# Both parts of z side by side in HBM and in the operand blocks, with block loads, stores and last rows in another order over the queues

## The chip, the cores and the metric

The kernel runs on one core of a Trainium2 chip. The metric is the device time of one execution in microseconds (us), as the median of several runs. Before the change it is 2041.6 us.

## What is computed

The reference first convolves x with h along the sequence, and then mixes tokens with two full matrices:

```python
Xf = np.fft.rfft(x, n=2 * S, axis=1); Hf = np.fft.rfft(h, n=2 * S, axis=0)
y = np.fft.irfft(Xf * Hf[None], n=2 * S, axis=1)[:, :S, :]      # x: (8, 5696, 128)
theta = y @ w_theta
zr, zi = y * np.cos(theta), y * np.sin(theta)
yr = np.einsum('ts,bsd->btd', w_tok_r, zr)                      # w_tok: (5696, 5696)
yi = np.einsum('ts,bsd->btd', w_tok_i, zi)
u = y + yr + yi
out = u + np.maximum(u @ w_ch, 0.0)
```

## The kernel before

**Stages.** From 0 to about 390 us of the span the convolution runs as a two-step FFT over eight groups (four pairs of batches, two halves of the channels). The token mixing follows. It takes up nearly all of the rest: TensorE multiplies transposed 128x128 pieces of w_tok with operand blocks of z that lie in SBUF, 512 columns (four batches of 128 channels) at a time.

**Phases.** A phase step (`phase_step`, which calls `phases_b`) takes one tile of 128 tokens and four batches. TensorE transposes y into the PSUM tile tpz (L688) and forms theta (L525 to L531); VectorE copies tpz into a place in the tile ring (L693), of which there are six; ScalarE makes the sine and the cosine (L536 to L538); VectorE makes the two products zi and zr (L549, L550), which lie side by side in one of seven tiles zz. The y tile is stored to y2_hbm (y_hbm in the profile, L694) and the products to z_hbm (L567, one DMA for every 64 tokens, 128 rows of 1024 bytes), or straight into an operand block (below). There are 22 steps for the first four batches, `steps0`, which run beside the end of the FFT, and 22 for the other four, `steps1`, which run between the first products of the mixing. Later tiles are worked off one by one beside the mixing ("background", `bg_phase`). There the two products lie in two tiles, red and mag, or c2 and c3, which also serve as accumulators, and are stored with two DMAs for every 64 tokens (L570).

**Operand blocks.** The tokens of a pass fall into 11 blocks j = 0 to 10. A block is a tile of 7 x 1024 bf16 per partition: four raw parts (M2, M6 of zr, M7, M5 of zi, each for one half q of the batches) and three sums (M3, M4, M1). Two further sums are made in place over M6 and M7 (`sum_ops`, L776, five VectorE operations of 128x1024 for each block). `load_b` reads a whole block with two DMAs, one for each part (L760), `load_b_half` the first half q of a block with two DMAs (L771). Block 0 lies in the tile ring, the others in pools that reuse the FFT's memory. For blocks 0 to 8 the half q = 0 comes by `load_b_half` from z_hbm, and the half q = 1 is written by `steps1` straight from zz to its home in the block (L563): even rows by a DMA on SP's queue, odd rows by a DMA on Pool's queue. Blocks 9 and 10 of the first pass come with `load_b` on SP's queue, once `steps1` is through (`open_mixing`). In the second pass all 11 blocks come with `load_b` on ScalarE's queue (ACT).

**Weights.** `load_w` brings a piece of w_tok with four DMAs on Pool's queue (L627) into one of six places in the tile ring; `pump` issues these loads as far as places are free. VectorE transposes the pieces (`w_t`, L838) and adds or subtracts some of them (`w_sum`, L847). `prepare` does that one stretch (up to three blocks) ahead of TensorE.

**Order.** A list scheduler sets the order of each engine's instructions by its own model of time, except where `manual_schedule` keeps an engine in program order: VectorE in the first pairs of both passes, and Pool (`late_order`) from the last FFT group to the half loads of blocks 0 to 6. These are called in one loop behind the FFT. After `late_order` closes, Pool's order is the scheduler's again.

**Pairs.** A pair is an output tile of each half of the rows. The first pairs of a pass are "classic": eight products of raw parts (L1167), pieces of which stand between the phase steps of `steps1`. The later pairs use seven products (M1 to M7, L1250) and add them into the accumulators c0 to c3 (L1257). The last 64 rows (tt None, L1137) are a narrow stage of four stretches. In the first pass it is second to last, in the second pass it comes second, right behind the first pair. There the sums of the blocks are made in step with the first pair: `safe` makes three of a block, `in_place` the other two; the ten of blocks 9 and 10 are made after the pair's last products and ahead of what `prepare` does for the second stretch of the last rows. Finished rows go through `u_stage` (ReLU branch, L915 to L930), which uses the single PSUM bank "misc" for the transposes (utp) and for the product (v), read by L927.

Of the kernel before, what the change touches and what calls it, by code (L numbers as in the profile page):

```python
# [23 lines left out]
def kernel(  # L24
# [20 lines left out]
    z_hbm_h = nc.dram_tensor("z_hbm", (2, 2, 11, 2, 4, 64, BD // 2), BF16, kind="Internal")  # L45
# [450 lines left out]
    def phases_b(ti, y_ap, b0, nb, yT, sb, th_pool, th_tag, zi_eng, turns=None, tags=("red", "mag"), m=P,  # L496
                 theta_ps=None, copy=None, home={}):
# [42 lines left out]
        if tags is None:  # L540
            k = zz_n[0] = (zz_n[0] + 1) % 7
            zz = fh.tile([P, 1024], F16, tag=f"hs{4 + k}", name="zz").bitcast(BF16).rearrange(
                "p (z n) -> p z n", z=2)
            zr, zi = zz[:, 0], zz[:, 1]
            sides["zz"] = zz
        else:
            zi = red.bitcast(BF16)[:, :n]
            zr = mag.bitcast(BF16)[:, :n]
# [4 lines left out]
        for e in range((m + 63) // 64):  # L553
# [7 lines left out]
            if tags is None and j in home:  # L561
                for r in range(2):
                    (nc.gpsimd if r else nc.sync).dma_start(  # L563
                        home[j][32 * i:32 * i + 32, :4096].rearrange("p (z q r n) -> p z q r n", z=2, q=2, r=2)[:, :, q_, r],
                        zz[e * 64 + r:e * 64 + 64:2])
            elif tags is None:
                nc.sync.dma_start(z_hbm[:, p_, j, q_, i].rearrange("z t n -> t z n"), zz[rows])  # L567
            else:
                for r, z in enumerate((zr, zi)):
                    nc.sync.dma_start(z_hbm[r, p_, j, q_, i], z[rows])  # L570
# [84 lines left out]
    def load_ya1(yt=None):  # L655
# [10 lines left out]
        else:  # L666
            for e in range(2):
                nc.gpsimd.dma_start(st[1][HD:, 2 + e, :],
                                    yt[64 * e:64 * e + 64].rearrange("p m n -> p (m n)")[:, :H])

    M2, M6, M7, M5, M1, M3, M4 = range(7)
    ORDER = (M3, M4, M5, M2, M1, M7, M6)
    home_of = {}

    def phase_step(ti, hh, store=nc.sync):
# [16 lines left out]
        def copy():  # L692
# [5 lines left out]
                 tags=None, copy=copy, home=home_of if hh else {})  # L698
# [15 lines left out]
    late_order = ExitStack()  # L714
# [28 lines left out]
    bpe = [ctx.enter_context(tc.tile_pool(name="bpool_e", bufs=1, side="right", reuse_waits="tile"))]  # L743
    bts_of = {0: [], 1: []}

    place_of = {}

    def new_b(j, pool):
        return ring["all"][:, WB:WB + BT] if j == 0 else pool.tile([P, BT], BF16, tag=f"b{j}", name=f"b{j}")

    def tile_b(p, j, pool):
        t_ = place_of.pop(j) if j in place_of else new_b(j, pool)
        bt = [t_[:, k * 1024:(k + 1) * 1024].rearrange("p (r n) -> p r n", r=2) for k in range(7)]
        bts_of[p].append(bt)
        return t_

    def load_b(p, j, pool, eng=nc.scalar):
        t_ = tile_b(p, j, pool)
        for z in range(2):
            sides["late"] = eng.dma_start(  # L760
                t_[:, z * 2048:(z + 1) * 2048].rearrange("p (q n) -> p q n", q=2),
                z_hbm[z, p, j].rearrange("q i (s r) n -> (i s) q (r n)", r=2))

    def home_pool(j):
        return bpe[0] if j < 7 else bpe[1] if j < NE else bp

    def load_b_half(j):

        t_ = home_of[j] = tile_b(0, j, home_pool(j))
        for z in range(2):  # L770
            nc.gpsimd.dma_start(t_[:, z * 2048:z * 2048 + 1024],  # L771
                              z_hbm[z, 0, j, 0].rearrange("i (s r) n -> (i s) (r n)", r=2))

# [18 lines left out]
    for j in range(7):  # L792
        load_b_half(j)
    for step in steps0:
# [8 lines left out]
    steps1 = [lambda ti=ti: phase_step(ti, 1, nc.gpsimd) for ti in  # L803
              [0, 5, 11, 16, 1, 6, 12, 17, 10, 21, 2, 7, 13, 18, 3, 8, 14, 19, 4, 15, 9, 20]]
# [3 lines left out]
    def open_mixing():  # L808
# [6 lines left out]
        load_b(0, NJ - 2, bp, nc.sync)  # L815
        sides["cs"] = [addend(0, n, t, h) for n, (t, h) in enumerate(((0, 1), (22, 0), (0, 0), (22, 1)))]
        load_b(0, NJ - 1, bp, nc.sync)
# [6 lines left out]
    def next_steps(n):  # L824
        for _ in range(min(n, len(steps1))):
# [3 lines left out]
            if not steps1:  # L829
                open_mixing()  # L830
# [482 lines left out]
```

## Time and profile before

| | us |
|---|---|
| median of 3 runs (2041.51 to 2042.7) | 2041.6 |
| the profiled execution | 2038.09 |
| its span, from first to last instruction | 2036.3 |
| PE busy in the span | 1948.2 |
| DVE (VectorE) busy | 1574.1 |
| POOL busy | 974.3 |
| ACT (ScalarE) busy | 654.7 |

The page of the profile counts an engine as busy while it executes instructions; DMA issues of SP and ACT are not in it, but those of Pool are. Its three DMA queues of interest are q0 (Pool's, 158.13 MB, 61.0% of the time of 16 DMA engines), q1 (SP's and ACT's, 140.25 MB, 24.1%) and q10 (11.54 MB, 1.6%). The granted clock of TensorE is 0.987 on average; in a stretch it is given as a share, 1.00 for full speed.

In the rows below, `L1167` is line 1167 of the kernel, `out<-in` names the tiles or tensors that an instruction writes and reads, `x6` counts the instructions merged into one row, and square brackets give the idle time before the first of them and what ended it.

### The profile page before, as it was taken

Reading aid. Unit: us, or ns where it says so; the run is one execution under the profiler, and the core shown is the slowest. Engines: PE = TensorE matmul, PEld = TensorE weight load, DVE = VectorE, ACT = ScalarE, POOL = GpSimd, SP = SyncE. Lnnn points to the kernel's source line nnn. Section 1 sums busy time; section 2 is a strip of 40 time slices with the busy share of each in tenths; the row PEclk is TensorE's granted clock in tenths of the full one; section 3 lists DMA queues with packets and bytes.
Section 4 is the critical chain, followed back from the end, with each engine's and each line's share of the span. In section 5 each row is a group of like instructions: output and inputs, shape, how many; then the busy total and the mean of one; then the engine's idle time right before and its main releaser. Section 6 shows DMA issues by size and latency. Waiting matters only on the chain.

```text
span 2036.3 us, 41470 instructions
## 1 busy us (share of the span) xinstructions
PE 1948.2 (96%) x15841; PEld 1074.5 (53%) x15841; DVE 1574.1 (77%) x2890; ACT 654.7 (32%) x1004; POOL 974.3 (48%) x1744
## 2 busy tenths in 40 slices
PE   5799999799999999999999998999999999999998
PEld 5688888654444444444444444444444444444444
DVE  8777778777788888888867668768677786777767
ACT  6788888862233323333300000111111111111111
POOL 8523321485353545454566454453544545354450
PEclk9899999899999999999999999999999999999999
DMA  9878975999798989999999799796977979788793
GB/s 117 62 84 124 88 83 167 255 268 186 161 174 179 174 171 167 181 167 181 165 176 154 117 251 220 127 154 125 154 134 138 155 128 154 129 153 140 133 156 85
DMA packets 491239, 312.56 MB, mean 153 GB/s; under 512 B 182983, under 2 KB 456007, under 8 KB 490055
## 3 DMA queue, kind: packets, MB, share of 16 engines
q0 software_dynamic: 322608, 158.13, 61.0%
q1 hardware_dynamic: 162448, 140.25, 24.1%
q10 hardware_dynamic: 5984, 11.54, 1.6%
q8 instruction: 124, 2.03, 0.4%
q14 instruction: 75, 0.61, 0.1%
HBM read 354.89 MB, written 90.82 MB: 219 GB/s over the span
## 4 chain that ended last, share of the span: by engine, by line
PE 67%; DVE 3%; DMA 3%; issue 1%; POOL 0%; ACT 0%; DVEq 0%; SPq 0%
PE m L1250 62%; DMA ring<-in_moe_w_tok_i_dram 2%; DVE c L1257 1%; PE utp L918 1%; PE v L925 1%; PE m L1254 1%; PE m L1137 1%; DVE b L776 1%; DVE wt L838 1%; PE tpz L866 0%; PE theta_ps L514 0%; POOL ring L627 0%; DMA wl<-in_moe_w_tok_i_dram 0%; DMA z_hbm<-mag 0%; DVE c L927 0%
## 5 line engine op out<-in xcount | busy, mean ns | idle before, releaser
L627 POOL DMA_DIRECT2D ring<-in_moe_w_tok_i_dram x720 | 388.2, 548 | 662.2 <-DVE wt L838 582.5
L627 POOL DMA_DIRECT2D ring<-in_moe_w_tok_r_dram x720 | 386.9, 549 | 122.6 <-DVE wt L838 64.2
L838 DVE STREAM_TRANSPOSE wt<-ring 128x384 f32<-128x384 f32 (+2 forms) x720 | 358.8, 523 | 103.2 <-PE m L1250 66.5
L1250 PE MATMUL m<-b,wt 128*128 128x512 bf16 x1640 | 388.4, 379 | 2.0 <-DVE wt L838 1.7
L1250 PEld LDWEIGHTS <-wt 128*128 128x128 bf16 x1804 | 176.0, 98 | 215.5 <-DVE wt L838 4.0
L1257 DVE TENSOR_TENSOR c<-c,m 128x512 f32<-128x512 f32 x412 | 265.3, 670 | 0.4 <-PE m L1250 0.4
L920 ACT ACTIVATE ring<-utp 128x512 bf16<-128x512 bf16 x85 | 50.8, 597 | 580.2 <-PE utp L918 580.2
L137 POOL DMA_DIRECT2D x<-in_x_dram x128 | 99.4, 798 | 141.5 <-PE ps L250 132.7
L420 PE MATMUL ps<-r_u,u_t 128*128 128x128 f16 x1024 | 125.2, 221 | 5.9 <-DVE u_t L400 2.9
L421 PE MATMUL ps<-r_v,v_t 128*128 128x128 f16 x1024 | 124.2, 220 | 0.3
L1167 PE MATMUL m<-b,wt 128*128 128x512 bf16 x480 | 112.8, 385 | 6.3 <-DMA b<-zz 2.8
L915 ACT ACTIVATE ub<-c 128x512 bf16<-128x512 f32 x88 | 55.1, 628 | 196.5 <-DMA ring<-in_moe_w_tok_i_dram 114.6
L421 PEld LDWEIGHTS <-v_t 128*128 128x128 f16 x1024 | 100.9, 99 | 5.2 <-issue 3.7
L420 PEld LDWEIGHTS <-u_t 128*128 128x128 f16 x1024 | 100.9, 99 | 3.9 <-DVE u_t L400 3.9
L398 ACT ACTIVATE xs<-ps 128x1024 f16<-128x1024 f32 x96 | 91.6, 983 | 9.6 <-PE ps L274 2.9
L400 DVE TENSOR_TENSOR u_t<-xs,hs 128x1024 f16<-128x1024 f16 x96 | 64.3, 670 | 32.1 <-ACT xs L398 29.9
L1167 PEld LDWEIGHTS <-wt 128*128 128x128 bf16 x528 | 51.1, 99 | 67.9 <-issue 4.8
L516 ACT ACTIVATE red<-theta_ps,magic 128x512 f32<-128x512 f32 (+1 forms) x46 | 31.6, 687 | 136.5 <-PE theta_ps L514 113.6
L268 PEld LDWEIGHTS <-w_t 64*128 64x128 f16 x3240 | 58.6, 100 | 23.6 <-issue 17.9
L868 ACT ACTIVATE ring<-tpz 128x512 bf16<-128x512 bf16 (+1 forms) x46 | 27.5, 597 | 130.8 <-PE tpz L866 113.7
L927 DVE SCALAR_TENSOR_TENSOR c<-v,c 128x512 f32<-128x512 f32 x88 | 59.9, 682 | 7.1 <-PE v L925 6.9
L400 DVE TENSOR_TENSOR v_t<-xs,hs 128x1024 f16<-128x1024 f16 x96 | 63.7, 664 | 0.0
(2934 smaller groups left out, 3816.1 us busy)
## 6 DMA issues: line engine op xcount, KB each, us to landing
ring<-in_moe_w_tok_r_dram POOLq DMA_DIRECT2D x352, 96.0 KB, 4.4
ring<-in_moe_w_tok_i_dram POOLq DMA_DIRECT2D x352, 96.0 KB, 4.7
ring<-in_moe_w_tok_r_dram POOLq DMA_DIRECT2D x352, 80.0 KB, 4.4
ring<-in_moe_w_tok_i_dram POOLq DMA_DIRECT2D x352, 80.0 KB, 3.9
cp_hbm<-c SPq DMA_DIRECT2D x88, 256.0 KB, 2.4
c<-cp_hbm SPq DMA_DIRECT2D x88, 256.0 KB, 4.5
out_dram<-c SPq DMA_DIRECT2D x88, 256.0 KB, 4.4
yy<-y_hbm SPq DMA_DIRECT2D x84, 128.0 KB, 2.4
```

Of the source, the lines that this page charges most:

```text
L137: nc.gpsimd.dma_start(x16[p0:p1, e, n0:n0 + 16, :HD], bass.AP(tensor=src.tensor, offset=src.offset + (p0 * N2 + n0) * D + dh * HD, ap=[[N2 ...
L268: nc.tensor.matmul(ps[:, e, j * HD:(j + 1) * HD], w_t2[rows, slot(e, c0 + j), N2 * (1 - ri):N2 * (3 - ri)], a_st["a"][rows, ri * K1 + c0 + ...
L398: nc.scalar.activation(xs[:, :, :, :ck], ps, AF.Copy)
L400: nc.vector.tensor_tensor(uv[r][:, :, :, c0:c0 + ck], xs[:, :, :, :ck], hv[:, r:r + 1].to_broadcast([P, 2, HD, ck]), op=mult)
L420: nc.tensor.matmul(o, u_t[:, at:at + P], r_u, start=True, stop=False)
L421: nc.tensor.matmul(o, v_t[:, at:at + P], r_v, start=False, stop=True)
L627: nc.gpsimd.dma_start(wb[32 * i:32 * i + 32, :ng, :nj * 64], bass.AP(tensor=a.tensor, offset=a.offset + row0 * S + p * H + i * QR + j0 * 6 ...
L838: nc.vector.transpose(wt.rearrange("p j t r -> p (j t r)").bitcast(F32).rearrange("p (j g t) -> p g j t", j=TJ, g=4)[:, :ng, :nj], wb[:, : ...
L927: nc.vector.scalar_tensor_tensor(c[:m], v[:m], 0.0, c[:m], op0=ALU.max, op1=ALU.add)
L1167: nc.tensor.matmul(ms[n // 2 * 2 + h], a[n][:, j, :, r], bts_of[p][jj][n % 2 * 2 + h][:, r, :], start=(n % 2 == 0 and jj == 0 and r == 0), ...
L1250: nc.tensor.matmul(ms[q], a[q][:, j, :, r], bts[jj][q][:, r, :], start=(jj == 0 and r == 0), stop=(jj == NJ - 1 and r == 1 and q not in left))
L1257: nc.vector.tensor_tensor(c, z, ms[q], op=op)
```

## The change

- z_hbm gets the two parts of a token side by side: rows of 2 x 512 bf16 (2048 bytes). A store of 64 tokens is one DMA with 64 such rows. An operand block holds its raw parts in the order (q, r, z, n) instead of (z, q, r, n); each raw part then is two runs of 512 with a distance of 1024. The background phases write both products into the tile red.
- `load_b` and `load_b_half` are one DMA each instead of two, with rows of 4096 bytes for every partition and half q. The even and the odd home rows of zz are 32 rows of 2048 bytes for each DMA.
- `load_b_half(0)` is called right behind the two ya loads of the last FFT group (in `load_ya1`), ahead of the yt stores; blocks 1 to 6 stay where they were.
- The first two steps of `steps1` store y on SP's queue instead of Pool's. The last of them sends its odd rows over ACT's queue.
- Pool is kept in program order (`pool_order`) from before `next_steps(2)` until `steps1` is through.
- `load_b` of blocks 9 and 10 goes over ACT's queue instead of SP's.
- In the second pass the ten sums of blocks 9 and 10 are made inside the first stretch of the last rows, behind `prepare` of the second one.

```diff
-    z_hbm_h = nc.dram_tensor("z_hbm", (2, 2, 11, 2, 4, 64, BD // 2), BF16, kind="Internal")
+    z_hbm_h = nc.dram_tensor("z_hbm", (2, 11, 2, 4, 64, 2, BD // 2), BF16, kind="Internal")
...
-            zr, zi = zz[:, 0], zz[:, 1]
             sides["zz"] = zz
         else:
-            zi = red.bitcast(BF16)[:, :n]
-            zr = mag.bitcast(BF16)[:, :n]
+            zz = red.bitcast(BF16).rearrange("p (z n) -> p z n", z=2)
+        zi, zr = zz[:, 0], zz[:, 1]
+        rows_of = zz.rearrange("p z n -> p (z n)")
...
                 for r in range(2):
-                    (nc.gpsimd if r else nc.sync).dma_start(
-                        home[j][32 * i:32 * i + 32, :4096].rearrange("p (z q r n) -> p z q r n", z=2, q=2, r=2)[:, :, q_, r],
-                        zz[e * 64 + r:e * 64 + 64:2])
-            elif tags is None:
-                nc.sync.dma_start(z_hbm[:, p_, j, q_, i].rearrange("z t n -> t z n"), zz[rows])
+                    (nc.sync if not r else odd_eng or nc.gpsimd).dma_start(
+                        home[j][32 * i:32 * i + 32, :4096].rearrange("p (q r w) -> p q r w", q=2, r=2)[:, q_, r],
+                        rows_of[e * 64 + r:e * 64 + 64:2])
             else:
-                for r, z in enumerate((zr, zi)):
-                    nc.sync.dma_start(z_hbm[r, p_, j, q_, i], z[rows])
+                nc.sync.dma_start(z_hbm[p_, j, q_, i].rearrange("t z n -> t (z n)"), rows_of[rows])
...
+            load_b_half(0)          # at the end of load_ya1(yt)
...
+        raw = t_[:, :4096].rearrange("p (q r z n) -> p q z r n", q=2, r=2, z=2)
+        bt = [raw[:, k % 2, 1 - k // 2] if k < 4 else
+              t_[:, k * 1024:(k + 1) * 1024].rearrange("p (r n) -> p r n", r=2) for k in range(7)]
...
-        for z in range(2):
-            sides["late"] = eng.dma_start(
-                t_[:, z * 2048:(z + 1) * 2048].rearrange("p (q n) -> p q n", q=2),
-                z_hbm[z, p, j].rearrange("q i (s r) n -> (i s) q (r n)", r=2))
+        sides["late"] = eng.dma_start(
+            t_[:, :4096].rearrange("p (q w) -> p q w", q=2),
+            z_hbm[p, j].rearrange("q i (s r) z n -> (i s) q (r z n)", r=2))
...
-        for z in range(2):
-            nc.gpsimd.dma_start(t_[:, z * 2048:z * 2048 + 1024],
-                              z_hbm[z, 0, j, 0].rearrange("i (s r) n -> (i s) (r n)", r=2))
+        nc.gpsimd.dma_start(t_[:, :2048], z_hbm[0, j, 0].rearrange("i (s r) z n -> (i s) (r z n)", r=2))
...
-    for j in range(7):
+    for j in range(1, 7):
         load_b_half(j)
...
-    steps1 = [lambda ti=ti: phase_step(ti, 1, nc.gpsimd) for ti in
-              [0, 5, 11, 16, 1, 6, 12, 17, 10, 21, 2, 7, 13, 18, 3, 8, 14, 19, 4, 15, 9, 20]]
+    order1 = [0, 5, 11, 16, 1, 6, 12, 17, 10, 21, 2, 7, 13, 18, 3, 8, 14, 19, 4, 15, 9, 20]
+    steps1 = [lambda ti=ti, n=n: phase_step(ti, 1, nc.sync if n < 2 else nc.gpsimd, nc.scalar if n == 21 else None)
+              for n, ti in enumerate(order1)]
...
-        load_b(0, NJ - 2, bp, nc.sync)
+        load_b(0, NJ - 2, bp)
...
-        load_b(0, NJ - 1, bp, nc.sync)
+        load_b(0, NJ - 1, bp)
...
             if not steps1:
+                pool_order.close()
                 open_mixing()
...
+                pool_order.enter_context(tc.manual_schedule(engines={mybir.EngineType.Pool}))
                 next_steps(2)
...
                 c_last = addend_last(p)
             a1, a2, sa = a
+            if p and first_of_pair:
+                for f in (safe, in_place):
+                    for j in range(3 * TJ, NJ):
+                        f(j)
...
-            elif turn == 3 * TJ:
-                for f in (safe, in_place):
-                    for j in range(3 * TJ, NJ):
-                        f(j)
```

More of the change, by code (lines that the diff above doesn't have):

```diff
@@ L496, in phases_b @@
     def phases_b(ti, y_ap, b0, nb, yT, sb, th_pool, th_tag, zi_eng, turns=None, tags=("red", "mag"), m=P,
-                 theta_ps=None, copy=None, home={}):
+                 theta_ps=None, copy=None, home={}, odd_eng=None):
         n = nb * D
@@ L669, in load_ya1, with new_b, tile_b, load_b @@
                                     yt[64 * e:64 * e + 64].rearrange("p m n -> p (m n)")[:, :H])
+            load_b_half(0)
+    bpe = []
+    bts_of = {0: [], 1: []}
+    place_of, home_of = {}, {}
+    def new_b(j, pool):
+        return ring["all"][:, WB:WB + BT] if j == 0 else pool.tile([P, BT], BF16, tag=f"b{j}", name=f"b{j}")
+    def tile_b(p, j, pool):
+        t_ = place_of.pop(j) if j in place_of else new_b(j, pool)
+        raw = t_[:, :4096].rearrange("p (q r z n) -> p q z r n", q=2, r=2, z=2)
+        bt = [raw[:, k % 2, 1 - k // 2] if k < 4 else
+              t_[:, k * 1024:(k + 1) * 1024].rearrange("p (r n) -> p r n", r=2) for k in range(7)]
+        bts_of[p].append(bt)
+        return t_
+    def load_b(p, j, pool, eng=nc.scalar):
+        t_ = tile_b(p, j, pool)
+        sides["late"] = eng.dma_start(
+            t_[:, :4096].rearrange("p (q w) -> p q w", q=2),
+            z_hbm[p, j].rearrange("q i (s r) z n -> (i s) q (r z n)", r=2))
+    def home_pool(j):
+        return None if j == 0 else bpe[0] if j < 7 else bpe[1] if j < NE else bp
+    def load_b_half(j):
+        t_ = home_of[j] = tile_b(0, j, home_pool(j))
+        nc.gpsimd.dma_start(t_[:, :2048], z_hbm[0, j, 0].rearrange("i (s r) z n -> (i s) (r z n)", r=2))
     M2, M6, M7, M5, M1, M3, M4 = range(7)
     ORDER = (M3, M4, M5, M2, M1, M7, M6)
-    home_of = {}
-    def phase_step(ti, hh, store=nc.sync):
+    def phase_step(ti, hh, store=nc.sync, odd_eng=None):
         st = sides["phases"]
@@ L697, in phase_step @@
         phases_b(ti, y_ap, 4 * hh, 4, yT, None, None, None, nc.vector, st["turns"], theta_ps=theta_ps,
-                 tags=None, copy=copy, home=home_of if hh else {})
+                 tags=None, copy=copy, home=home_of if hh else {}, odd_eng=odd_eng)
     tile_order = []
@@ L712, in with_load @@
         return both
-    late_order = ExitStack()
+    late_order, pool_order = ExitStack(), ExitStack()
     for g, (bp, dh) in enumerate(groups):
@@ L741 @@
     conv.close()
[L743 to L758, printed above, removed]
-        for z in range(2):
-            sides["late"] = eng.dma_start(
-                t_[:, z * 2048:(z + 1) * 2048].rearrange("p (q n) -> p q n", q=2),
-                z_hbm[z, p, j].rearrange("q i (s r) n -> (i s) q (r n)", r=2))
[L764 to L769, printed above, removed]
-        for z in range(2):
-            nc.gpsimd.dma_start(t_[:, z * 2048:z * 2048 + 1024],
-                              z_hbm[z, 0, j, 0].rearrange("i (s r) n -> (i s) (r n)", r=2))
+    bpe.append(ctx.enter_context(tc.tile_pool(name="bpool_e", bufs=1, side="right", reuse_waits="tile")))
     def sum_ops(bt):
```

## The prediction

> **What bounds the kernel now.** I read the page first, then the stretches of 20 us, then TensorE's waits, then the time lines of single engines around the worst stretches.
>
> ```profile
> span 2036.3 us, 41470 instructions
> PE 1948.2 (96%) x15841; PEld 1074.5 (53%) x15841; DVE 1574.1 (77%) x2890; ACT 654.7 (32%) x1004; POOL 974.3 (48%) x1744
> ```
>
> TensorE is the bound: 88 us of the span are not PE. From 560 to 1160 us and from 1300 us on every stretch shows 20.00 of 20 at clock 1.00, and nothing that the change touches there can shorten it. The gain must come out of a few stretches (columns: us, then busy us and instructions of PE, PEld, DVE, ACT, POOL; granted clock, DMA share, GB/s):
>
> ```profile
> 380.00:400.00 20.00, 12.89 (x130) 9.24 (x128) 15.92 (x31) 17.38 (x31) 8.04 (x15) 0.90 0.82 207
> 400.00:420.00 20.00, 18.66 (x146) 11.29 (x145) 14.77 (x28) 13.80 (x24) 14.32 (x27) 0.85 0.98 343
> ...
> 440.00:460.00 20.00, 15.07 (x73) 6.57 (x70) 13.76 (x26) 3.48 (x7) 16.47 (x31) 0.93 0.96 243
> 460.00:480.00 20.00, 19.98 (x103) 9.37 (x102) 12.52 (x24) 3.43 (x7) 8.17 (x16) 0.98 1.12 247
> ...
> 1240.00:1260.00 20.00, 17.62 (x97) 7.85 (x95) 18.75 (x36) 2.78 (x5) 9.60 (x18) 1.00 0.84 177
> 1260.00:1280.00 20.00, 17.16 (x114) 7.82 (x115) 12.63 (x28) 1.79 (x3) 12.67 (x24) 0.91 0.93 155
> ```
>
> What TensorE waits for in them (us in total, times, longest):
>
> ```profile
> PE m L1137 <- DVE out__18362 L847: 4.1, 1, 4.1
> ...
> PE m L1167 <- DMA b<-zz: 2.8, 1, 2.8
> PE m L1167 <- DMA ring<-z_hbm: 2.6, 1, 2.6
> PE m L1167 <- DVE wt L838: 2.1, 1, 2.1
> ```
>
> The single engines say why. Pool first (start, us), then VectorE:
>
> ```profile
> 386.89 1.06 POOL L452 DMA_DIRECT2D yt_hbm<-yt  x2
> 387.94 1.12 POOL L771 DMA_DIRECT2D ring<-z_hbm  x2
> 396.02 0.55 POOL L694 DMA_DIRECT2D y_hbm<-ring  x1 [6.96 <-DVE ring L693]
> 396.60 3.20 POOL L771 DMA_DIRECT2D b<-z_hbm  x6
> ```
> ```profile
> 412.99 0.42 DVE L693 COPY ring<-tpz 128x512 bf16<-128x512 bf16 x1 [1.12 <-DMA y_hbm<-ring]
> ...
> 442.54 0.42 DVE L693 COPY ring<-tpz 128x512 bf16<-128x512 bf16 x1 [1.68 <-DMA y_hbm<-ring]
> ...
> 545.94 0.69 DVE L1257 TENSOR_TENSOR c<-yy,m 128x512 f32<-128x512 bf16 x1 [1.55 <-DMA z_hbm<-mag]
> ...
> 1255.69 6.10 DVE L776 TENSOR_TENSOR b<-b 128x1024 bf16<-128x1024 bf16 x10
> 1261.71 0.62 DVE L838 STREAM_TRANSPOSE wt<-ring 128x192 f32<-128x192 f32 x2
> ```
>
> To be seen: block 0's half stands behind the yt stores; blocks 1 to 6 stand behind a y store for which Pool sat 6.96 us; the ten sums of blocks 9 and 10 stand ahead of the transposes that the last rows need.
>
> **The change, part by part.** Four places (A to D) carry the sum.
>
> *A, 387 to 413 us: half loads of block 0 earlier, blocks 1 to 6 one DMA each, the first two y stores on SP.* Block 0's load would be issued at 386.9, ahead of the yt stores, as one DMA of 0.54 us instead of two. It now lands at 398.48, when TensorE resumes, 10 us after issue; the ya loads issued just ahead of it (385.84) landed at 392.08, 6 us after. At 6 us it lands near 393, before TensorE runs out of work at 395.83. Blocks 1 to 6 save 6 x 0.54 = 3.2 us of Pool and start near 389. That removes 2.65 us and the 1.25 us wait on block 1 behind it, and perhaps the clock loss after 398 (0.15 x 20 = 3.0 us): upper end 6.9 us. Then what is late next? VectorE's copy at 412.99 waits for a y store on SP, and the transposes of step 7 (413.47) start 0.06 us after that copy's end. Unless that store lands earlier, nothing of the 6.9 us survives step 7: lower end 0. The store is issued on SP at 403.06, behind some seven z stores of 0.57 us and more each. Full-size stores with rows of 2048 bytes (cp_hbm) take 0.32 to 0.43 us of SP. A z store with 2048-byte rows saves about 0.25 us, and 7 x 0.25 = 1.75 us. I take **1.5 us** (0 to 6.9). The two y stores added to SP (0.65 us each) are queued behind that store; behind them on SP stand even home rows, which TensorE reads only from the second half of the blocks on, some 14 steps later.
>
> *B, 440 to 461 us: Pool in program order, 2 loads for blocks 7 and 8 instead of 4, the last step's odd rows on ACT, blocks 9 and 10 loaded over ACT.* Pool idles 2.48 us at 425.67 ahead of a y store and then falls behind: the copy of step 20 waits 1.68 us at 442.54 for a y store, the transposes behind it start at 444.27, and TensorE waits 2.1 us. The last odd rows leave Pool at 449.99 to 451.05, though VectorE made them by 447.9; TensorE waits 2.8 us for them until 457.16, and the clock is low after it (0.07 + 0.02 of 20 us = 1.8 us). With the order fixed Pool loses the 2.48 us, two loads (1.1 us) and the last two rows (1.1 us), 4.7 us in all against a lag of 3 to 7. So step 20's copy comes about 1.6 us earlier (gain 1.7 of the 2.1), and the last rows leave ACT by 447.5; ACT is empty then (it sits 26 us until 469.64). At the 6 us that they take now they land by 453.5; TensorE would need them at 454.35 - 1.7 = 452.6, so 2.0 of 2.8 us go. With a wait under 1 us the 1.8 us of clock go too. 1.7 + 2.0 + 1.8 = 5.5; I take **5 us**. Low end 2, only the copy's wait; high end 2.1 + 2.8 + 1.8 = 6.7. The ACT queue's waits for block 9's room hold nobody up, for nothing is queued behind them before 469.
>
> [...]
>
> *C, 540 to 555 us: both parts written into red, one store for two.* In background steps the tile mag is free when the product is done instead of after its own store. At 545.94 VectorE waits 1.55 us for just that store, and TensorE then sits 1.05 and 0.43 us. Against that, red's store starts one product (0.69 us) later and red becomes c2, needed two sums (1.3 us) later. Between 0 and 1.5; **1 us**.
>
> *D, 1254 to 1275 us: ten sums behind the next transposes.* Now: sums 1255.69 to 1261.7, transposes and sum of the second last-row stretch until 1262.7, TensorE idle 4.05 us, then 0.09 x 20 = 1.8 us of clock. After: that stretch's operands are ready at 1256.9, so TensorE runs it from 1258.65 to 1261.3; the sums end near 1263; then comes the ReLU sum (L927, 0.68) and the third stretch's transposes, ready near 1264.6, against a start at 1268.11 now. That is 3.5 us earlier, less up to 1.8 if the clock falls for a gap of 3.3 us: **2.5 us**. Lower end 0: the bank misc is shared, and its reader L927 stands behind the ten sums, so if TensorE's transposes into misc are queued ahead of the second stretch, it stops at 1258.6 as now. Upper end 4.05 + 0.65 = 4.7.
>
> *At nothing:* the sums' operands become two runs of 512 instead of one of 1024. L400 makes 1024 elements in runs of 8 in 664 to 670 ns against 647 to 686 for L776, so I see no cost. Matmuls keep their 512 contiguous columns (379 ns). Pass 2's eleven block loads move the same bytes as before; TensorE is full from 1180 to 1240, which covers them (the fourth rival prices it without that cover).
>
> Sum: 1.5 + 5 + 1 + 2.5 = **10 us**, off a profiled execution of 2038.1 us (span 2036.3). The median is 3.5 us higher, which I take as unchanged: 2041.6 - 10 = **2031.6**.
>
> **The rivals.**
> 1. *D is empty*, because of misc: gain 7.5, 2034. For: TensorE's rows at 1263.38 show the utp transposes among the first matmuls of that stretch. Against: the order there was one matmul first, so the list follows readiness. Chance 0.12.
> 2. *A and B are given back*: VectorE waits 5.2 us for weights at 468.63, and the DMA share is 1.12 in 460 to 480. If the weights come no earlier, the first pair runs into them and C + D = 3.5 remain, 2038: no change. Against: TensorE did not stop there (19.98 of 20). Chance 0.13.
> 3. *The sums slow down* (slower): at the rate of L1257 (512 elements in 0.61 us, start to start) 1024 would take about 1.1 us instead of 0.62, say +0.45 us for each of 110. In 1220 to 1262 VectorE is full (19.87 of 20), so 55 x 0.45 = 25 us reach TensorE; with the others, 2041.6 - 7.5 + 25 = 2059. It decides from 0.14 us a sum. L400 speaks against. Chance 0.06.
> 4. *Weights starve in 1190 to 1250* (slower): block rows of 4096 instead of 2048 bytes. Pool's weight DMAs are spaced 1.2 us there against 0.54 alone, so block rows take 0.66 of it. If the queues alternate by rows, that doubles: 1.86 us. The block loads now last 60 us and would last 46; 25 weight DMAs fall in it, 25 x 0.66 = 16.5 us late, less some 4.5 us between transposes and use: 12 us, with D lost: 2041.6 - 7.5 + 12 = 2046. It decides from 1.68 us a DMA. Against: rows of 2048 and 4096 may be cut alike, and VectorE waited only 1.28 us for weights there. Chance 0.09. [...]
>
> **How the numbers follow.** The forecast case has 0.60; its own range is 2024 (most of A, B and D) to 2037.5 (B's and D's low ends). With rivals 1 and 2 it becomes 2024 to 2041, leaving out rivals 3 and 4 (0.15) and a little below. 0.2% is 4.1 us, about what a measurement of this kernel tells from no change. Faster: 0.95 of 0.60, 0.9 of 0.12 and a sixth of 0.13, 0.70. Same: the rest of these, 0.15. Slower: 0.15.
>
> **What would show it.** Right: no wait of PE for ring<-z_hbm near 398 and none for b<-zz near 456; Pool's half loads of blocks 1 to 3 near 389 to 391; clock 1.00 in 460 to 480; no VectorE wait for z_hbm<-mag; L776's ten sums behind transposes of 128x192 near 1256, and the third last-row stretch some 3.5 us earlier against the end of the pair before. Wrong: step 7's transposes no earlier than 413 (A = 0), L776 above 0.8 us (rival 3), weight DMAs spaced above 1.7 us (rival 4), or a PE wait on weights near 470 (rival 2).

## The result, and the profile after

The changed kernel takes 2050.96 us (median of 6 runs, 2049.38 to 2052.81) against 2041.55 us for the kernel before (6 runs, 2037.5 to 2042.7): a ratio of 1.0052, 95% interval 1.0041 to 1.0063. It is slower by some 10 us, where 10 us less were forecast, and outside the forecast's range. The two profiled executions (2052.81 and 2038.09 us) lie on opposite sides of their medians, so the traces show 14.7 us, of which some 5 us are variation from run to run.

The page of the kernel after, its stretches of 20 us (columns as before) and TensorE's waits:

```profile
span 2051.0 us, 41108 instructions
...
PE 1942.5 (95%) x15664; PEld 1076.4 (52%) x15841; DVE 1574.7 (77%) x2890; ACT 655.4 (32%) x1004; POOL 967.8 (47%) x1731
```
```profile
400.00:420.00 20.00, 16.05 (x126) 9.74 (x126) 13.15 (x25) 12.17 (x22) 11.22 (x21) 0.91 0.94 325
440.00:460.00 20.00, 19.34 (x111) 9.42 (x111) 16.18 (x30) 5.88 (x11) 13.10 (x25) 1.00 0.91 241
460.00:480.00 20.00, 11.61 (x51) 5.11 (x50) 10.87 (x20) 2.77 (x5) 10.18 (x19) 0.74 1.09 210
1220.00:1240.00 20.00, 14.99 (x61) 6.33 (x61) 10.97 (x21) 0.00 (x0) 4.36 (x8) 0.91 1.10 353
1240.00:1260.00 20.00, 17.96 (x83) 8.03 (x83) 19.92 (x37) 0.00 (x0) 9.54 (x18) 1.00 0.89 189
1260.00:1280.00 20.00, 17.37 (x111) 8.05 (x109) 19.71 (x38) 2.78 (x5) 11.31 (x22) 1.00 0.77 98
```
```profile
PE tpz L865 <- DMA yT<-yt_hbm: 8.3, 1, 8.3
...
PE m L1171 <- DVE wt L837: 7.1, 3, 5.0
...
PE tpz L715 <- DVE ring L720: 3.8, 2, 2.0
PE tpz L715 <- DMA ya<-yt: 3.5, 1, 3.5
...
PE utp L917 <- DVE c L926: 2.2, 1, 2.2
```

440 to 460 us came out as forecast (19.34 us of TensorE where there were 15.07). But 460 to 480, full before, lost 8.4 us and a quarter of its clock, and 1220 to 1240, which was full before, lost 5 us:

```profile
1220.00:1240.00 20.00, 20.00 (x94) 9.09 (x93) 19.87 (x35) 0.00 (x0) 7.39 (x14) 1.00 1.14 324
```

Two waits head the list of those in the mixing: one of 8.3 us for yT, and three for weights, of which two (6.9 us in all) stand in pass 2's first pair, where TensorE had no wait before. (Lines move by the change: transposes of a step L688 are now L715, the background's transposes L866 are L865, the classic products L1167 are L1171, weight loads L627 are L624, weight transposes L838 are L837, the sums L776 are L773.)

Placed by the start of the same instructions in both traces, the 14.7 us are made up as follows (us; a plus is a loss):

| stretch | before | after | difference |
|---|---|---|---|
| start to the first transpose of `steps1` | 390.0 | 391.0 | +1.0 |
| the 22 steps, first to last transpose | 50.8 | 52.4 | +1.6 |
| last transpose to the first M1 to M7 product | 70.5 | 75.6 | +5.0 |
| from there to the last rows of pass 1 | 659.5 | 660.0 | +0.5 |
| pass 2's first product to the end of its first pair | 38.5 | 47.1 | +8.6 |
| from there to the first M1 to M7 product | 21.5 | 19.5 | -2.0 |

The rest is equal to 0.1 us. The first row shows no effect of the change: over the traces of all kernels here the steps start anywhere between 387.5 and 394.0 us, with and without the change's parts. So there are two large losses to explain, one in each pass.

**Pass 1.** TensorE's time line of the kernel after, where the 8.3 us stand:

```profile
459.63 1.89 PE L1171 MATMUL m<-b,wt 128*128 128x512 bf16 x8 [0.20 <-DMA b<-z_hbm]
469.86 0.60 PE L865 MATMUL tpz<-ident_bf,yT 128*128 128x128 bf16 x4 [8.34 <-DMA yT<-yt_hbm]
470.26 5.21 PE L1171 MATMUL m<-b,wt 128*128 128x512 bf16 x12
```

Four small transposes of background work stand in the queue ahead of the products of block 10, whose load lands at 463.60, and wait for a yT load that is issued at 455.66 and lands at 469.81. In the kernel before they stood behind these products, and yT landed later still, at 470.88:

```profile
473.51 0.39 PE L866 MATMUL tpz<-ident_bf,yT 128*128 128x128 bf16 x4
```

Nothing in the diff names them. But their load is called under `tc.issue_after(sides["late"].ins)`, and `sides["late"]` is the last `load_b`. That order binds instructions of one engine. The yT loads are on SP, and so were the loads of blocks 9 and 10; now those are on ACT, and the order binds nothing. The scheduler then takes yT to be early and places its transposes early.

**Pass 2.** Pool's weight loads and VectorE's wait for them in the kernel after, then Pool in the kernel before, some 12 us after the first product in both:

```profile
1230.88 0.55 POOL L624 DMA_DIRECT2D ring<-in_moe_w_tok_i_dram  x1 [1.57 <-DMA ring<-in_moe_w_tok_i_dram]
1233.36 0.54 POOL L624 DMA_DIRECT2D ring<-in_moe_w_tok_i_dram  x1 [1.94 <-DMA ring<-in_moe_w_tok_i_dram]
1235.53 0.55 POOL L624 DMA_DIRECT2D ring<-in_moe_w_tok_i_dram  x1 [1.62 <-DMA ring<-in_moe_w_tok_i_dram]
```
```profile
1235.37 2.42 DVE L837 STREAM_TRANSPOSE wt<-ring 128x384 f32<-128x384 f32 x5 [8.99 <-DMA ring<-in_moe_w_tok_i_dram]
```
```profile
1226.24 0.54 POOL L627 DMA_DIRECT2D ring<-in_moe_w_tok_i_dram  x1 [0.31 <-DMA ring<-in_moe_w_tok_i_dram]
1227.48 0.54 POOL L627 DMA_DIRECT2D ring<-in_moe_w_tok_i_dram  x1 [0.69 <-DMA ring<-in_moe_w_tok_i_dram]
1228.70 0.54 POOL L627 DMA_DIRECT2D ring<-in_moe_w_tok_i_dram  x1 [0.68 <-DMA ring<-in_moe_w_tok_i_dram]
```

The spacing goes from 1.2 to 2.2 us and more, and the transposes of the weights wait 8.99 us. The DMA queues in the 20 us from the first product on, before and then after (packets, MB, share of the time of 16 engines). q0 has the weights. q10 is ACT's queue, here with the block loads: ACT issues nothing but pass 2's 22 block loads in the kernel before, and they are the 11.54 MB of q10. So q1 is SP's queue alone.

```profile
DMA packets 4888, 6.36 MB, mean 318 GB/s; under 512 B 427, under 2 KB 2483, under 8 KB 4887
...
q10 hardware_dynamic: 2057, 3.97, 56.0%
q0 software_dynamic: 2065, 1.19, 40.1%
```
```profile
DMA packets 3669, 6.95 MB, mean 348 GB/s; under 512 B 357, under 2 KB 1874, under 8 KB 3668
...
q10 hardware_dynamic: 1118, 4.28, 53.7%
q0 software_dynamic: 1454, 0.89, 29.5%
```

A block packet took 0.56 x 320 us / 2057 = 87 ns before and 0.537 x 320 / 1118 = 154 ns after (119 and 73 packets of 4 bytes are counted among them; over all of pass 2's block loads a packet of a full row took 92.8 and 170.0 ns on average). The engines move more in all, 348 GB/s instead of 318, but a quarter less of the weights. Most of the surplus is not block rows (4.28 MB instead of 3.97) but SP's queue, 1.76 MB instead of 1.18, mainly copies of accumulators (c and cp_hbm).

### The profile page after: what moved, and what is told of

Read it like the earlier page. It is cut to its first block, busy times and chain, and to the rows that moved or that the text cites. A ratio compares the mean times of both kernels' runs of the same rounds, so it can differ in the third digit from the quotient of the medians.

```text
span 2051.0 us, 41108 instructions
## 1 busy us (share of the span) xinstructions
PE 1942.5 (95%) x15664; PEld 1076.4 (52%) x15841; DVE 1574.7 (77%) x2890; ACT 655.4 (32%) x1004; POOL 967.8 (47%) x1731
## 4 chain that ended last, share of the span: by engine, by line
PE 68%; DMA 4%; DVE 4%; issue 2%; POOL 1%; ACT 0%; SPq 0%; DVEq 0%; ACTq 0%
PE m L1250 60%; PE m L1171 3%; DMA ring<-in_moe_w_tok_i_dram 3%; DVE c L1257 2%; PE v L924 1%; PE utp L917 1%; PE m L1254 1%; DVE wt L837 1%; DMA yT<-yt_hbm 1%; POOL ring L624 1%; PE theta_ps L514 0%; PE tpz L865 0%; PE m L1141 0%; DMA ring<-in_moe_w_tok_r_dram 0%; DVE b L773 0%
## 5 line engine op out<-in xcount | busy, mean ns | idle before, releaser
L624 POOL DMA_DIRECT2D ring<-in_moe_w_tok_i_dram x720 | 388.7, 546 | 659.2 <-DVE wt L837 574.2
L624 POOL DMA_DIRECT2D ring<-in_moe_w_tok_r_dram x720 | 387.7, 546 | 135.9 <-DVE wt L837 69.4
L837 DVE STREAM_TRANSPOSE wt<-ring 128x384 f32<-128x384 f32 (+2 forms) x720 | 358.9, 523 | 119.9 <-PE m L1250 66.5
L919 ACT ACTIVATE ring<-utp 128x512 bf16<-128x512 bf16 x85 | 50.8, 597 | 578.8 <-PE utp L917 578.8
L1171 PE MATMUL m<-b,wt 128*128 128x512 bf16 x465 | 113.2, 390 | 3.2 <-DVE wt L837 2.2
L1171 PEld LDWEIGHTS <-wt 128*128 128x128 bf16 x528 | 51.6, 100 | 67.4 <-DVE wt L837 8.6
```

Of the source, the lines that this page charges most:

```text
L624: nc.gpsimd.dma_start(wb[32 * i:32 * i + 32, :ng, :nj * 64], bass.AP(tensor=a.tensor, offset=a.offset + row0 * S + p * H + i * QR + j0 * 6 ...
L837: nc.vector.transpose(wt.rearrange("p j t r -> p (j t r)").bitcast(F32).rearrange("p (j g t) -> p g j t", j=TJ, g=4)[:, :ng, :nj], wb[:, : ...
L1171: nc.tensor.matmul(ms[n // 2 * 2 + h], a[n][:, j, :, r], bts_of[p][jj][n % 2 * 2 + h][:, r, :], start=(n % 2 == 0 and jj == 0 and r == 0), ...
```

## The experiments

Theories: **T1**, rows of 4096 bytes in pass 2's block loads take DMA time from the weights; its rival R1, the same bytes at another time. **T2**, the lost order puts the yT transposes ahead of the products; its rival R2, slow transfers. **T3**, formed after the first four runs: a block now arrives as a whole, while before half of it was enough for the first products. "Stretch" is pass 2's first product to its first pair's end (38.5 us before, 47.1 after). Each kernel was timed in 5 rounds beside the kernel before, whose medians were 2039.5 to 2040.9 us; the ratios to it are what is compared.

**1. Blocks 9 and 10 back on SP.**

```diff
-        load_b(0, NJ - 2, bp)
+        load_b(0, NJ - 2, bp, nc.sync)
...
-        load_b(0, NJ - 1, bp)
+        load_b(0, NJ - 1, bp, nc.sync)
```

> The changed kernel with one thing put back: the loads of blocks 9 and 10 in pass 1 go over SP's queue again, so that the order written for the background work (behind the last of these loads, on the same engine) holds again for the yT loads. Theory T2 (order): in the changed kernel PE stood 8.3 us at 461 to 470 on yT transposes (L865) that are queued ahead of the products of blocks 9 and 10, and ran at a clock of 0.74 in 460 to 480; with the chain back, the wait is gone, PE is busy over 19 us of 460 to 480 at a clock near 0.98, and the kernel takes 11 to 13 us less than the changed one: 2038 to 2040, about the time of before. Rival R2 (the yT load is merely slowed by other transfers, of rows of 4096 bytes, whatever the order): a wait of some 8 us stays in 455 to 480 and the time stays within 3 us of 2051. In both, pass 2's first pair keeps its loss (1215 to 1254 in before) of about 8.6 us.

Measured: 2048.89 us, ratio 1.0039 (1.0025 to 1.0052). The wait on yT is gone and pass 1 ends 5.8 us earlier, but the time falls by 2.1 us where 11 to 13 were expected; by its time alone the run would speak for R2. In the trace TensorE now waits 3.5 us for block loads and 2.3 us for weights in the same place (460 to 480: 15.03 of 20 at clock 0.83), and the stretch is 48.3 us. T2's cause is there; undoing it in this way only uncovers the next wait.

**2. Rows of 2048 bytes in pass 2.**

```diff
-        sides["late"] = eng.dma_start(
-            t_[:, :4096].rearrange("p (q w) -> p q w", q=2),
-            z_hbm[p, j].rearrange("q i (s r) z n -> (i s) q (r z n)", r=2))
+        for c_ in range(2 if p else 1):
+            w_ = slice(c_ * 2048 // 2, (c_ + 1) * 2048 // 2) if p else slice(0, 2048)
+            sides["late"] = eng.dma_start(t_[:, :4096].rearrange("p (q w) -> p q w", q=2)[:, :, w_], z_hbm[p, j].rearrange("q i (s r) z n -> (i s) q (r z n)", r=2)[:, :, w_])
```

> The changed kernel with each block load of pass 2 cut into two DMAs whose rows are 2048 bytes long instead of one with rows of 4096; the bytes, the queue and the order stay. Theory T1 (rows): block rows and weight rows take turns on the engines, so a weight row waits 171.7 ns behind a 4096-byte row and 92.8 ns behind a 2048-byte one; the weight DMAs of 1220 to 1250 come back from 2.1 to 2.5 us apart to about 1.2, the PE wait m<-wt goes, and the kernel takes 7 to 9 us less: 2042 to 2044. Rival R1 (the same bytes at the same time in the same order, so the row length does nothing; the loss comes from the loads starting at another time): spacing stays over 2 us and the time within 2 us of 2051.

Measured: 2046.89 us, ratio 1.0032 (1.0018 to 1.0047). R1 falls: no TensorE wait on weights is left in 1215 to 1260, the four weight loads of a piece start 0.5 to 1.6 us apart until 1244, and 1220 to 1240 is full again (19.89 of 20). The time is 3 us above what was expected: the stretch is 43.5 us, 3.6 less, not 8.6 less, because another wait has come up (TensorE's waits from 1215 to 1300):

```profile
PE m L1171 <- DMA b<-z_hbm: 3.3, 2, 2.9
```

The clock is 0.91 behind it (1240 to 1260), which is 1.7 us lost. The 3.3 us of waits and these 1.7 us are the 5.0 us by which the stretch is still longer than before.

**3. The four transposes ordered behind the products.** The loads stay on ACT.

```diff
-                with tc.issue_after(sides["late"].ins) if p == 0 and tt == 1 else ExitStack():
+                with tc.issue_after(sides["mm"].ins) if p == 0 and tt == 1 else ExitStack():
...
-                    nc.tensor.matmul(ms[n // 2 * 2 + h], a[n][:, j, :, r],
+                    sides["mm"] = nc.tensor.matmul(ms[n // 2 * 2 + h], a[n][:, j, :, r],
```

> The changed kernel with its loads as they are (blocks 9 and 10 over ACT's queue), but the four background transposes of 460 to 470 are ordered behind the products of blocks 9 and 10 on PE; nothing else moves on PE. Theory T2 (order): the 8.3 us wait and the low clock behind it go, 11 to 13 us less than the changed kernel, 2038 to 2040, the same as with the loads put back on SP. Rival: what costs the time is the move of the loads to ACT itself (ACT's work or the loads' landing), and the transposes only show it; then PE waits for ring or b instead and the time stays within 3 us of 2051.

Measured: 2042.32 us, ratio 1.0014 (1.0002 to 1.0027), 2 us above what was expected. TensorE's time line where the 8.3 us were:

```profile
462.45 2.75 PE L1171 MATMUL m<-b,wt 128*128 128x512 bf16 x12 [1.83 <-DMA b<-z_hbm]
...
471.10 0.39 PE L865 MATMUL tpz<-ident_bf,yT 128*128 128x128 bf16 x4
```

460 to 480 has 18.06 us at clock 1.00, and last transpose to first M1 to M7 product takes 67.7 us (75.6 after, 70.5 before). Pass 2's first product starts at 1215.1, as before. The yT loads land no earlier than 468 here too, so it is the order and not the transfer: T2 stands, R2 falls, and T2 is worth 7.9 us of the trace.

**4. The repairs of 1 and 2 together.**

> Both repairs at once: blocks 9 and 10 over SP's queue in pass 1, and 2048-byte rows in pass 2. T1 and T2 are in different stages (460 to 480, and 1215 to 1254), so their gains should add: about 20 us under the changed kernel, 2029 to 2033, which would be 8 to 12 us under before: near what the rest of the change was forecast to bring. If the two losses share a cause or one is only put off, the sum is under 15 us and the time at or over that of before (2041.5).

Measured: 2045.96 us, ratio 1.0030 (1.0017 to 1.0042). They don't add: the wait for block loads stays in pass 1 (460 to 480: 14.77 at 0.83) and in pass 2 (4.6 us, stretch 44.5).

**5 and 6. Half blocks first.** In 5 the loads of pass 2 are cut by q, the half of the first products first, with rows of 4096 bytes; in 6 each half is cut again into rows of 2048. The lines added in 6:

```diff
+        for q, w in ([(slice(1 - k // 2, 2 - k // 2), slice(k % 2 * 1024, k % 2 * 1024 + 1024)) for k in range(4)] if p else [(slice(0, 2), slice(0, 2048))]):
+            sides["late"] = eng.dma_start(t_[:, :4096].rearrange("p (q w) -> p q w", q=2)[:, q, w],
+                z_hbm[p, j].rearrange("q i (s r) z n -> (i s) q (r z n)", r=2)[:, q, w])
```

> The changed kernel with each block load of pass 2 cut into two DMAs, the half that the first products read (q = 1) first; the rows stay 4096 bytes long. Theory T3 (half blocks): before, the first half of a block's load was enough for the products k = 0 and 1; now one load brings the whole block, so the first product of a block waits for all of it, and the load waits until all of the block is free. This alone should start the loads about 1.2 us earlier and take the PE wait on b away, but leave the weights starved: weight DMAs still 2 us and more apart in 1220 to 1250 and the wait m<-wt still 5 us or more. The first pair's loss against before stays at 7 to 10 us. If the rows were not the cause, it would fall under 3 us.

> The changed kernel with each block load of pass 2 cut into four DMAs: the half of q = 1 first, and rows of 2048 bytes. T1 and T3 together say that the first pair of pass 2 is then as in before: no PE wait on wt and none over 1 us on b, weight DMAs about 1.2 us apart, and the stretch from pass 2's first product to its first pair's end at 38.5 to 40 us (47.1 in the changed kernel, 38.5 before, 43.5 with rows of 2048 alone). The kernel takes 2041 to 2044, the loss of pass 1 (8 us) still in it. Rival: what is left after the shorter rows (5 us) is not the half blocks but the ten sums taken out of their old place, or the clock; then the stretch stays at 43 us or more.

Measured: 2049.21 us, ratio 1.0047 (1.0029 to 1.0066), and 2047.75 us, ratio 1.0035 (1.0023 to 1.0047). The stretches are 45.8 and 43.8 us. With long rows the weights still starve (4.5 us of TensorE, weight loads about 2 us apart); T1 holds. With short rows the halves bring nothing over run 2 (43.5): TensorE waits 3.3 us for block loads, now in three parts. T3 as stated fails here, but this cut also doubles the number of DMAs.

**7 and 8. Both repairs, and A undone.** 7 is 3 with the loads of 6. In 8, besides, `load_b_half(0)` goes back into the loop of blocks 0 to 6, and all of `steps1` store y over Pool's queue; the single load for a block, which A has as well, stays.

> Both losses repaired: the four background transposes of pass 1 ordered behind the products of blocks 9 and 10 (loads of blocks 9 and 10 left on ACT), and pass 2's block loads in four DMAs, q = 1 first, rows of 2048. The stage gains should add: 8 us in pass 1 and 7 to 8.5 us in pass 2, so 2034 to 2037, under before by 4 to 7 us; the rest of the change (the last step's order, the later sums) is then what gains. If the time is at or over that of before, the remaining parts bring nothing.

> The kernel with both repairs, and part A of the change undone: the half load of block 0 goes back behind the opening of the blocks, and the first two stores of y go over Pool's queue again. By the forecast's step A this costs 1.5 us (0 to 6.9) against the kernel with both repairs; by the changed kernel's trace, in which the second step's y lands 2.7 us later and PE waits 3.5 us for it, undoing A gains 1 to 2 us. The stretch from the first to the last transpose of the mixing phase's 22 steps, 50.8 us before and 50.4 to 52.8 in the kernels with A, tells it.

Measured: 2041.93 us, ratio 1.0010 (0.9998 to 1.0021), and 2040.27 us, ratio 0.9998 (0.9986 to 1.0010). The gains add in part (3 and 6 apart had won 0.0038 and 0.0017, here it is 0.0042), and what is left of the change gains nothing over the kernel before. Undoing A does not cost 1.5 us; it tends to gain, though the intervals overlap. The 22 steps take 51.7 and 51.0 us. In the stretch from the first M1 to M7 product to pass 1's last rows every kernel of the new layout with A needs 659.6 to 660.3 us, and the two without A (8 and 10) 658.5 and 658.1: TensorE's waits there, in 7 and then in 8, differ in one line by more than 0.2 us:

```profile
PE theta_ps L514 <- ACT ring L867: 2.0, 2, 1.7
```
```profile
PE theta_ps L514 <- ACT ring L867: 0.3, 1, 0.3
```

This wait is 1.6 to 2.2 us in all nine kernels with A and 0.3 us in all seven without it. How A leads to it is not shown.

**9. D alone, on the kernel before.** The ten sums move as in the change, nothing else.

> The kernel before with part D of the change alone: the ten sums of blocks 9 and 10 come behind the next stretch's weight transposes. The forecast's step D says 2.5 us less (0 to 4.7); the changed kernel's trace shows 2.0 us gained after the first pair's end. So 2036 to 2040.5, and the stretch from pass 2's first product to its first pair's end stays at 38.5 us. Rival: the 5 us that stay in that stretch when both repairs are made (43.5 to 46.3 in place of 38.5) come from D; then the stretch is 43 us or more here, and the kernel is 2 to 4 us slower than before.

Measured: 2038.39 us, ratio 0.9981 (0.9968 to 0.9995): the fastest of all, faster than both kernels. VectorE (lines as in the kernel before), then TensorE:

```profile
1253.81 0.63 DVE L838 STREAM_TRANSPOSE wt<-ring 128x192 f32<-128x192 f32 x2
1254.48 0.36 DVE L847 TENSOR_TENSOR out__18352<-wt 128x384 bf16<-128x384 bf16 x1
1254.75 6.10 DVE L776 TENSOR_TENSOR b<-b 128x1024 bf16<-128x1024 bf16 x10
1260.77 0.68 DVE L927 SCALAR_TENSOR_TENSOR c<-v,c 128x512 f32<-128x512 f32 x1
```
```profile
1261.51 0.58 PE L918 MATMUL utp<-ident_bf,ub 128*128 128x128 bf16 x4 [2.75 <-DVE c L927]
```

The transposes stand ahead of the sums, the wait of 4.05 us has become one of 2.75, and the last rows start and end sooner (end of the pair to first M1 to M7 product 20.4 us instead of 21.5 in the profile). The stretch is 39.1 us, so D does not take the 5 us.

**10. Kernel 8 with D undone.**

> The kernel with both repairs and A undone, and D undone too: the ten sums in their old place. If D takes the 5 us that stay in pass 2's first pair, the stretch goes back to 38.5 to 40 us and the stretch behind it (the last rows) grows by about 2 us: 2036 to 2038. If D does not, the stretch stays at 43.5 to 44.5 and the time rises by about 2 us to 2041 to 2043: then the loads of the blocks themselves (their rows in the other layout, or the weights that run ahead of them) are late.

Measured: 2042.08 us, ratio 1.0007 (0.9993 to 1.0021), stretch 44.3 us, TensorE's wait of 4.9 us in the last rows is back. D is cleared from this side too.

**11 and 12. B alone, order mended, in the old layout; and B with D.** Edits as in the change's B and in 3, on the kernel before.

> The kernel before, in its own layout of z, with part B of the change alone and its order mended: Pool's program order, the odd rows of the last step and the loads of blocks 9 and 10 on ACT, and the four background transposes of pass 1 behind the products of blocks 9 and 10. The forecast's step B says 5 us less (2 to 6.7). The kernels with B and the mended order gained 0.8 to 2.8 us between the last step's transpose and pass 1's first full product, so that 1 to 3 us is likelier: 2037 to 2040.

> B (order mended) and D together in the old layout of z. If the gains add, 3 to 5 us less than before: 2035 to 2037.5, and faster than every kernel so far. If the layout was what paid for them, or if one only uncovers the next wait, it is within 2 us of before.

Measured: 2048.30 us, ratio 1.0031 (1.0018 to 1.0044), and 2046.62 us, ratio 1.0024 (1.0011 to 1.0036). They are 8 and 9 us above the upper ends of what was expected. TensorE and ACT's queue in 11:

```profile
464.33 3.26 PE L1169 MATMUL m<-b,wt 128*128 128x512 bf16 x8 [4.41 <-DMA b<-z_hbm]
472.45 1.86 PE L1169 MATMUL m<-b,wt 128*128 128x512 bf16 x4 [4.85 <-DMA b<-z_hbm]
```
```profile
450.37 14.49 ACTq L760 DMA_DIRECT2D b<-z_hbm  x4
```

In the old layout blocks 9 and 10 are four loads. The fourth left ACT only at 464.49, 0.2 us after the third had landed, and landed at 472.40. In the changed kernel they are two, issued at 450.64 and 453.79. So B's move to ACT does not pay in these two kernels without the change's single loads. What held the fourth back is not shown. The stretch in the old layout is 41.3 and 39.5 us.

**13. Whole blocks in the old layout.** The kernel before, with its two loads of a block cut by q and not by z, so that the first product needs both.

> The kernel before with one thing changed: each block load of pass 2 is still two DMAs with rows of 2048 bytes, but they bring the halves by q and not by z, so that the first product of a block needs both of them. If waiting for the whole block (T3) is what takes the 5 us that the shorter rows did not give back, the stretch from pass 2's first product to its first pair's end goes from 38.5 (39.1 and 39.5 in the two other kernels with the old loads and later sums) to 43 us or more, PE waits over 3 us for b<-z_hbm, and the kernel takes 4 to 5 us more than before, 2044 to 2046. If the new layout itself makes the loads late, the stretch stays under 41 us and the time within 2 us of before.

Measured: 2040.61 us, ratio 1.0005 (0.9994 to 1.0015), stretch 41.4 us, 2.9 us of waits for b<-z_hbm. By the stretch it falls between the two expectations, by the time it is the second. Nor can the 2.9 us be put down to whole blocks: with the loads as before, TensorE waits 2.5 us for blocks in run 11 (stretch 41.3), 0.6 us in 9 and 0.9 us in 12.

**14. Rows of 1024 bytes in pass 2.** As 2, with four loads for each block.

> The changed kernel with pass 2's block loads cut into four DMAs with rows of 1024 bytes. T1 as sharing: block rows and weight rows take turns, so the row's length sets what part of the DMA engines' time the blocks get. With 4096 bytes the eleven blocks were in 51.8 us after the first issue and the weights starved; with 2048 in 61.8 us and PE waited 3.3 us for blocks. With 1024 the weights should never be late (no PE wait on wt) and the blocks later still, 68 us or more after the first issue, so that PE waits 8 us or more for b<-z_hbm and the stretch is 48 us or more: slower than with 2048, 2049 to 2054. If the row's length matters to the weights alone, the stretch stays at 43 to 44.5 and the time at 2046 to 2048.

Measured: 2052.76 us, ratio 1.0063 (1.0051 to 1.0076), as expected from T1: no wait on weights, and TensorE waits for blocks (waits from 1205 to 1300, then the queues in the first 20 us):

```profile
PE m L1171 <- DMA b<-z_hbm: 8.4, 5, 4.1
```
```profile
DMA packets 6856, 5.82 MB, mean 291 GB/s; under 512 B 586, under 2 KB 6814, under 8 KB 6854
...
q10 hardware_dynamic: 4373, 4.21, 69.5%
q0 software_dynamic: 2151, 1.24, 42.2%
```

| rows of pass 2's blocks, new layout | 4096 (after) | 2048 (run 2) | 1024 (run 14) |
|---|---|---|---|
| blocks in, after the first issue (us) | 51.8 | 61.8 | 69.2 |
| blocks, weights in the 20 us before the first product (MB) | 5.73, 1.02 | 4.58, 1.50 | 3.52, 1.82 |
| blocks, weights in the 20 us from it (MB) | 4.28, 0.89 | 4.05, 1.21 | 4.21, 1.24 |
| SP's queue in these (MB) | 1.76 | 1.05 | 0.34 |
| all queues in these (GB/s) | 348 | 316 | 291 |
| TensorE waits on weights, on blocks (us) | 6.9, 0 | 0, 3.3 | 0, 8.4 |
| stretch (us) | 47.1 | 43.5 | 51.0 |

The DMA engines are full around the first product: in the stretches of 20 us from it the queues' shares add up to 110 to 117% of 16 engines' time, in the 20 us ahead of it to 110% in the changed kernel, and 1200 to 1220 has a DMA share of 1.20 in run 14. In these three kernels the longer rows bring the blocks sooner and take it from the weights, most of all before the first product; the shorter rows feed the weights and bring the blocks late. Behind the first product the blocks get nearly the same in all three kernels, and SP's queue takes part in the sharing too.

**What stays open.** Of the stretch's 8.6 us, 3.6 are the rows' length (run 2). Of the other 5.0 us, D takes none (9, 10); in run 2 they are 3.3 us of waits for block loads and 1.7 us of low clock behind them. The other kernels add up alike. The six with the new layout and rows of 2048 bytes wait 3.3 to 6.1 us for blocks, each lost 1.7 us by the granted clock, and have stretches of 43.5 to 46.3 us (the sum fits to 0.4 us). The five with the old layout wait 0 to 2.9 us, lose no clock, and have 38.5 to 41.4. In the first the last block lands 36.3 to 39.1 us after pass 2's first product, in the second 33.9 to 36.7. Why blocks come later in the new layout, with the same bytes in rows of the same length, is not settled. Waiting for whole blocks is a candidate that is not shown: it took no more than 2.9 us in the old layout (13), and getting halves first gave nothing back in the new one (6).

## Why the prediction was wrong, point by point

The sum put down gains of 1.5 us for A, 5 for B, 1 for C and 2.5 for D, and nothing for pass 2's block loads. Between the two traces the stretch of B lost 5.0 us and pass 2's first pair 8.6: together 18.6 us away from the sum, of the 19.4 between forecast and measured median. D's stretch gained 2.0 and the steps, where A was to gain, lost 1.6.

- **B is the step that failed first.** "The ACT queue's waits for block 9's room hold nobody up, for nothing is queued behind them" costed the move of the two loads by what stands behind them on the new queue. What counted was what the old queue held behind them: the background's order hung on their being on SP. Without it four transposes stopped TensorE for 8.3 us (run 3: 7.9 us in all). B's own mechanism came: no wait on b<-zz near 456, 19.34 of 20 us. But its term was too large: with the order mended, last transpose to first M1 to M7 product is 0.7 to 2.8 us shorter than before (3, 7, 8, 10) where 5 us were put down (2 to 6.7), for TensorE then waits for block loads and weights a little later (3.7 us in run 3).
- **"At nothing": pass 2's block loads.** The cover named was a full TensorE from 1180 to 1240. It lasted only as long as the weights came in time; this is the **fourth rival**, given 0.09. It priced 12 us and a spacing of 1.86 us; measured are 8.6 us and 2.2 us. Rows of 2048 and 4096 are not cut alike (87 and 154 ns for a packet): that argument against it was wrong. Its turns of one row each, which T1 assumes in the expectations of 2 and 14 too, fit the packets before (2057 of blocks, 2065 of weights), in run 2 (2102 and 2116) and in the changed kernel's 20 us ahead of the first product (1485 and 1484), but neither those of the 20 us from it (1118 and 1454) nor run 14's (4373 and 2151); how an engine chooses between queues is not shown. What it missed is that shorter rows are no cure by themselves.
- **A** brought nothing, and in the traces it lost; the times of 7 and 8 do not resolve it. PE's wait on ring<-z_hbm near 398 went, as forecast, and the half loads of blocks 1 to 4 left Pool at 389.5 to 391.2. But the second ya load, now with the half loads right behind it, landed 7.4 us after its issue instead of 5.7, and TensorE waited 3.5 us for it instead of 1.7 (this load takes 6.2 to 7.8 us in the nine kernels with A, 4.9 to 6.1 in the others). Step 7's transposes start at 414.96 us (413.47 before), so nothing survived that step, which was A's lower end; and the kernels with A lose up to 1.7 us more in the background work (the wait of L514 in 7 and 8), below that end. The 22 steps take 50.4 to 52.8 us with A and 50.6 to 51.7 without, so the steps themselves tell no gain.

```profile
387.92 0.56 POOL L697 DMA_DIRECT2D ring<-z_hbm  x1
388.47 1.06 POOL L452 DMA_DIRECT2D yt_hbm<-yt  x2
389.52 2.23 POOL L697 DMA_DIRECT2D b<-z_hbm  x4
400.45 1.13 POOL L697 DMA_DIRECT2D b<-z_hbm  x2 [8.70 <-DMA yt_hbm<-yt]
```

  On Pool in the kernel after, blocks 5 and 6 even wait 8.70 us.
- **C**: VectorE's wait for z_hbm<-mag is gone, and so is TensorE's wait of 1.0 us for a sum (L847) near 552: all five kernels of the old layout have it (0.8 to 1.0 us), none of the new one. The kernels of the new layout without A need 1.0 to 1.4 us less than before for the rest of pass 1 (658.1 and 658.5 against 659.5), about the 1 us put down. C was not run by itself, and that A's loss hides it in the changed kernel is argued from these numbers.
- **D** was right in kind and about right in size: 2.5 us forecast, 2.0 between the traces (and between those of 8 and 10), 1.1 in the last rows of run 9's trace, and 2.5 between the medians of run 9, whose interval is wide (0.05 to 0.32%, 1 to 6.5 us).
- **Rival 3** (slow sums) did not come: ten sums take 6.10 us in both kernels. **Rival 1** is seen as a remnant: the transposes into misc wait 2.2 to 2.75 us behind the ten sums, but only after the second stretch of the last rows. **Rival 2** pointed at 460 to 480 for another reason than the one that struck first; its wait for weights is there in run 1 (2.3 us).
- **The clock.** A gap of 2.86 us in run 2 stands ahead of a stretch (1240 to 1260) at 0.91, one of 2.75 us in run 9 ahead of one (1260 to 1280) at 0.83, but one of 2.7 us in run 7 in a stretch (500 to 520) at 1.00 and one of 2.86 us in run 13 (up to 454.4) in stretches (440 to 480) at 1.00, so the length of a gap alone does not decide. In the traces' records of the granted clock each fall from 380 to 1300 us is to half speed and lasts 3.41, 6.83 or 10.24 us; the shortest costs 1.7 us. That a wait under 1 us costs no clock, on which B's 1.8 us rested, was the author's estimate; in the kernel before, a wait of 1.05 us (up to 552.14) stands in a stretch (540 to 560) at 1.00.

## What to carry to other kernels

When an instruction is moved to another queue, look up who is ordered after it: an order that holds within one engine only is lost, and the diff does not show it (here TensorE stopped for 8.3 us). With the DMA engines full, the length of the block rows changed here what the weights got (0.89, 1.21 and 1.24 MB in 20 us beside rows of 4096, 2048 and 1024 bytes), so price a change of the row's length by the queue that it shares with, and from both sides. Run the parts of a change one by one: here the one small edit that touched no layout (D) was the only one shown to pay by itself; B alone, in the old layout, cost 0.3% (run 11).

## What was not expected of the hardware

The 20 us from pass 2's first product, with the 16 DMA engines full (117, 114 and 110% by the queues' shares), run at 291, 316 and 348 GB/s with block rows of 1024, 2048 and 4096 bytes, and yet the stretch is shortest at 2048 (51.0, 43.5 and 47.1 us): the sum of the bytes is not what TensorE waits for here. And the excess of pass 2's first stretch over 38.5 us is, in every kernel with a single fall of the clock, the waits and 1.7 us for that fall, to 0.4 us: a wait of 3.3 us for blocks costs 5.0 us (run 2).
